# A gated mix of attention and a state-space convolution on one core: wide Toeplitz loads, paired lag steps, 32-channel tables

## The chip, the core and the metric

The kernel runs on one core of one Trainium2 chip. A core has a matrix engine (TensorE, PE in the profile; its weight loads are listed apart as PEld), a vector engine (VectorE, DVE), a scalar engine (ScalarE, ACT), GpSimd (POOL), a queue engine that issues the transfers (SyncE, SP), and 16 DMA engines between HBM and the on-chip memory SBUF, which has 128 partitions. TensorE writes to PSUM, eight banks of 512 float32 columns in each partition. The metric is device time in microseconds of one launch.

## The reference: what is computed

Two branches read the same input x (2048 tokens of 448 channels, bfloat16) and are mixed by a gate of one number per token.

```python
def _A_ref(x, wq, wk, wv, wo):            # attention, 16 heads of 28, one K and one V for all heads
    q = (x @ wq).reshape(B, S, H, Dh).transpose(0, 2, 1, 3)
    k = x @ wk
    v = x @ wv
    scores = einsum("bhqd,bkd->bhqk", q, k) * (Dh ** -0.5)
    p = softmax(scores, axis=-1)
    o = einsum("bhqk,bkd->bhqd", p, v)
    return o.transpose(0, 2, 1, 3).reshape(B, S, H * Dh) @ wo

def _B_ref(u, A_re, A_im, B_re, B_im, C_re, C_im, log_dt, Dskip):   # state-space convolution
    dt = exp(log_dt)[:, None]
    logdA = dt * (A_re + 1j * A_im)       # 448 channels x 256 modes
    dB = dt * (B_re + 1j * B_im)
    P = exp(logdA[:, :, None] * arange(L))
    K = einsum("dn,dnl,dn->dl", C_re + 1j * C_im, P, dB).real   # a kernel of 2048 lags per channel
    y = causal_convolution(u, K)          # by FFT in the reference
    return y + u * Dskip

g = sigmoid((x * gate_w).sum(-1, keepdims=True))
out = g * A_ref(x, ...) + (1 - g) * B_ref(u, ...)
```

In the kernel both branches take their input from x (`A_x`), as the reference does: `b = _B_ref(x, ...)`.

## The kernel before

The program is a list of operations with costs that its author estimated; a scheduler in the kernel file orders them at build time, one fixed order for each engine. Attention is a stream of 1024 score tiles (128 keys x 512 queries of one head). Tiles are scored in batches of three and two alternately, in two halves of three PSUM banks; one exp of ScalarE handles a batch; P.V follows per batch, each head in its own 32-column strip of TensorE, and V carries a column of ones that yields the denominator.

```python
        def qk(b):                       # scores of batch b (3 or 2 tiles), then exp
            for k, (qc, g, kt, h) in enumerate(ts):
                e.matmul(psS[1536 * s + 512 * k : +512], kT[32 * h : +29, 128 * kt : +128], qT[32 * h : +29, ...],
                         tile_position=(32 * h, 0))
            activation(expT[1536 * es], psS[1536 * s], AF.Exp, scale=SQ)                 # "L915" in the profile
        def pv(b):                       # P.V of batch b
            for k, (qc, g, kt, h) in lst:
                e.matmul(psB[32 * h : +32], vaug[32 * kt : +32], expT[1536 * es + 512 * k],
                         start=(kt == 0), stop=(kt == 15), tile_position=(0, 32 * h))    # "L929"
        # ... [cut] order of the program: pv(b), then qk(b + 2)
```

The SSM works on chunks of 16 channels. `masters` squares the mode multipliers z (float32), `tables` builds on VectorE powers of z by doubling (five levels) and, by a sixth step, tables for the second half of the lags; `kgen` multiplies the tables on TensorE into 2048 lags of each channel, which go to an HBM scratch `KP_scratch`. From there each group of four channels comes back as a Toeplitz operand T, a megabyte in two transfers of 64 partitions, in a ring of three buffers. The convolution takes 16 lag steps for each of four channels, each step one matmul of 64 columns:

```python
    def tload(self, gi):
        pg.dma([(self.T.v(64 * h, 64, s * 4096, [[1, 4096]]),
                 dram(self.KP, 4 * gi * KPW + 4096 * h, [[4, 64], [1, 4096]])) for h in range(2)],
               (128, 8192), f"T{s}", rd=[("KP", c), "pad"], wr=[("T", s)], pr=1)
    def conv(self, c):
        for k in range(4):
            self.tload(4 * c + k)
            for m_ in range(16):
                for j in range(4):
                    e.matmul(ps.v(32 * j, 32 - m_, po + 64 * k, [[1, 64]]),
                             self.U.v(0, P, m_ * D + 4 * gi + j, [[D, 32 - m_]]),
                             self.T.v(0, P, s * 4096 + (960 - 64 * m_) * 4 + j, [[4, 64]]),
                             start=(m_ == 0), stop=(m_ == 15), tile_position=(0, 32 * j))   # "L820"
        # ... [cut] one VectorE product by (1 - g) into cst, transposes to token order, added to O ("L828", "L797", "L804")
    def tables(self, c):                 # 28 chunks; per level three products/sums of 4*w*32 elements
        for lv in range(5):
            tensor_tensor(dst3, src, mbf_re, mult)      # "L725"
            tensor_tensor(tmp, src, mbf_im, mult)       # "L728"
            tensor_tensor(dst, dst, tmp, add)           # "L733"
        # then three of 2048 elements for the other half ("L741", "L743", "L748")
```

The gate is computed as a row in all partitions, `grow` = g and `omg` = 1 - g over 2048 tokens. P.V results are multiplied by g as they leave PSUM (`norm`, "L874"); the denominators go through three small transfers (SBUF to SBUF, to HBM, and back as a broadcast) for a reciprocal on 128 partitions. The skip term is x scaled in place by Dskip and 1 - g on VectorE (`bx`, "L837") and added by identity matmuls in the output projection ("L855").

Of the kernel before, what the change touches and what calls it, by code (L numbers as in the profile page):

```python
# [20 lines left out]
CH = 16  # L21
NCH = D // CH
HC = 2 * CH
KPW = 2112
SQ = 1.0 / math.sqrt(DH)
# [28 lines left out]
class Prog:  # L54
# [12 lines left out]
    def op(self, eng, fn, ns, rd=(), wr=(), pr=0, lat=60, lock=None, unlock=None, comm=None):  # L67
# [5 lines left out]
        if comm is not None:  # L73
            deps[self.lastw[comm]] = 1
            self.commops.setdefault(comm, []).append(o.i)
# [36 lines left out]
    def schedule(self):  # L112
# [19 lines left out]
        while done < n:  # L132
            best = None
            for e in ENG:
                T = free[e]
                for i in ready[e]:
                    o = ops[i]
                    r = max(rt[i], T)
                    if o.lock is not None:
                        L = locks.setdefault(o.lock, [None, 0.0, []])  # L140
                        if L[0] is not None:
                            continue
                        r = max(r, L[1])
                    if o.comm in comm:
                        r = max(r, ops[comm[o.comm]].end)
                    key = (r, o.pr, i)
                    if best is None or key < best[0]:
                        best = (key, e, i)
# [10 lines left out]
            if o.comm is not None:  # L159
                if o.comm in comm:  # L160
                    o.deps[comm[o.comm]] = 1
                comm[o.comm] = i
# [124 lines left out]
class Kernel:  # L287
# [10 lines left out]
    def build(self):  # L298
        nc = self.nc
        with self.es:  # L300
# [6 lines left out]
            self.prep_attn()  # L307
# [5 lines left out]
    def alloc(self):  # L313
# [13 lines left out]
        self.GW = sb("GW", NT * P, BF)  # L327
        self.Wb = sb("Wb", P, BF)
        self.ident = sb("ident", P, BF)
        self.absq = sb("absq", 2 * 512, BF)  # L330
        self.qT = sb("qT", 3 * 512, BF)
        self.expT = sb("expT", 3 * 1536, BF)
        self.acc = sb("acc", 2 * 512, F32)
        self.rdenB = sb("rdenB", 512, F32)
        self.denT = sb("denT", 2 * 16, F32)
        self.onT = sb("onT", 8 * 512, BF)
        self.grow = sb("grow", S, BF)
        self.omg = sb("omg", S, BF)
        self.omq = sb("omq", 64, F32)
        self.anti = sb("anti", P, BF)  # L340
        self.U = sb("U", 32 * D, BF)
        self.O = sb("O", 16 * D, BF)
        self.tab = sb("tab", 2 * 6 * 32 * HC, BF)
        self.tmp = sb("tmp", 2 * 2048, BF)
        self.NTR = 3
        self.T = sb("T", self.NTR * 4096, BF)
        self.NB = 7
        self.BC = NCH // self.NB
        self.LV = 256
        self.MC = 5 * 256 + 128  # L350
        self.mbf = sb("mbf", 2 * self.BC * self.MC, BF)
        BW = self.BC * HC
        self.BW = BW
        self.mst = sb("mst", 2 * 2 * BW, F32)
        self.msq = sb("msq", 2 * BW, F32)
        self.sgn = sb("sgn", 8, F32)
        self.seedz = sb("seedz", 2 * 2 * D, F32)
        self.seedw = sb("seedw", 2 * 2 * D, BF)
        self.dt32 = sb("dt32", D, BF)
        self.kstg = sb("kstg", 2 * 256, BF)  # L360
        self.cst = sb("cst", 2 * 256, BF)
        self.small = sb("small", 32, F32)
        self.smallb = sb("smallb", 16, BF)
# [3 lines left out]
    def consts(self):  # L367
        pg = self.pg
        V = lambda b, off, n: b.v(0, P, off, [[1, n]])
        pg.op("pool", lambda e: e.memset(V(self.ident, 0, P), 1.0), 200, wr=["id"])  # L370
# [3 lines left out]
        sm = self.small  # L374
        pg.op("dve", lambda e: e.tensor_reduce(V(sm, 0, 1), self.ident.v(0, P, 28, [[32, 4]]), AX.X, ALU.max),
              100, rd=["id"], wr=["s0"])
        pg.op("dve", lambda e: e.tensor_scalar(V(sm, 1, 1), V(sm, 0, 1), -0.5, 0.5, ALU.mult, ALU.add),
              100, rd=["s0"], wr=["s1"])
        pg.op("dve", lambda e: e.tensor_scalar(V(sm, 2, 1), V(sm, 0, 1), 0.5, 0.5, ALU.mult, ALU.add),
              100, rd=["s0"], wr=["s2"])  # L380
        pg.op("dve", lambda e: e.memset(V(sm, 3, 1), 0.5 * math.pi), 60, wr=["hpi"])
        for c, val in enumerate([-1.0, 1.0, 1.0, -1.0]):
            pg.op("pool", lambda e, c=c, val=val: e.memset(V(self.sgn, c, 1), val), 60, wr=["sgn"])
        ms = lambda buf, n, val, key: pg.op("dve", lambda e: e.memset(V(buf, 0, n), val), 60 + n / 3.8, wr=[key])
        ms(self.Wq, NT * 512, 0.0, "Wq")
        ms(self.Wk, NT * P, 0.0, "Wk")
        pg.op("dve", lambda e: e.memset(self.Wk.v(96, 32, 3 * P + 28, [[32, 4]]), 1.0), 60, wr=["Wk"])
        pg.op("dve", lambda e: e.memset(self.Wk.v(96, 16, 3 * P + 28, [[32, 4]]), 0.0), 60, wr=["Wk"])
        pg.op("dve", lambda e: e.memset(self.xT.v(96, 32, 3 * S, [[1, S]]), 1.0), 600, wr=["xT3a", "xT3b"])
        ms(self.Wo, NT * D, 0.0, "Wo")  # L390
        ms(self.Wb, P, 0.0, "Wb")
        pg.op("dve", lambda e: e.memset(self.vaug.v(0, P, 28, [[32, 16]]), 1.0), 80, wr=["va"])
        pg.op("dve", lambda e: e.memset(self.vaug.v(0, P, 29, [[32, 16], [1, 3]]), 0.0), 80, wr=["va"])
        pg.op("dve", lambda e: e.memset(self.U.v(0, 64, 16 * D, [[1, 16 * D]]), 0.0), 2000, wr=["Uz"])
        an = self.anti.v(0, 32, 0, [[32, 4], [1, 32]])
        pg.op("pool", lambda e: e.memset(an, 1.0), 100, wr=["anti"], pr=4)
        pg.op("pool", lambda e: e.affine_select(out=an, in_=an, compare_op=ALU.is_equal, fill=0.0, base=-31,
                                                pattern=[[0, 4], [1, 32]], channel_multiplier=1), 300,
              rd=["anti"], wr=["anti"], pr=4)
        pg.op("dve", lambda e: e.memset(V(self.kstg, 0, 256), 0.0), 100, wr=[("kst", 0)])  # L400

    def loads(self):
        pg, ins = self.pg, self.ins
        xst = self.tab
        x = ins["A_x"]
        for hf in range(4):
            pg.dma([(xst.v(0, P, hf * 4 * D, [[D, 4], [1, D]]), dram(x, hf * 4 * P * D, [[D, P], [P * D, 4], [1, D]]))],
                   (512, 896), f"x{hf}", wr=[("xst", hf)], eng="sp")
        raw = self.O
        self.names = ["B_A_re", "B_A_im", "B_B_re", "B_B_im", "B_C_re", "B_C_im"]  # L410
        wst = self.acc.cast(BF)
        wks = self.rdenB.cast(BF)

        def lraw(k):
            pg.dma([(raw.v(0, DT, k * 1024, [[NM, 4], [1, NM]]), dram(ins[self.names[k]], 0, [[NM, DT], [DT * NM, 4], [1, NM]]))],
                   (448, 512), f"raw{k}", wr=[("raw", k)])
        pg.dma([(wks.v(0, DT, 0, [[DH, 4], [1, DH]]), dram(ins["A_wk"], 0, [[DH, DT], [DT * DH, 4], [1, DH]])),
                (self.Wv.v(0, DT, 0, [[32, 4], [1, DH]]), dram(ins["A_wv"], 0, [[DH, DT], [DT * DH, 4], [1, DH]]))],
               (896, 56), "wk", wr=["wks", "Wv"])
        pg.op("dve", lambda e: e.tensor_copy(self.Wk.v(0, DT, 0, [[32, 16], [1, DH]]),  # L420
                                             wks.v(0, DT, 0, [[DH, 4], [0, 4], [1, DH]])), 300, rd=["wks"], wr=["Wk", "rd"])
        lraw(0)
        lraw(1)
        pg.dma([(self.dt32.v(0, P, 0, [[1, D]]), dram(ins["B_log_dt"], 0, [[0, P], [1, D]]))], (128, 896), "ldt", wr=["dt"])
        pg.dma([(wst.v(0, DT, 0, [[D, 4], [1, D]]), dram(ins["A_wq"], 0, [[D, DT], [DT * D, 4], [1, D]]))],
               (448, 896), "wq", wr=["wqs"])
        pg.op("dve", lambda e: e.tensor_copy(self.Wq.v(0, DT, 0, [[32, 64], [1, DH]]),
                                             wst.v(0, DT, 0, [[DH, 64], [1, DH]])), 1000, rd=["wqs"],
              wr=["Wq", ("acc", 0), ("acc", 1)])
# [3 lines left out]
        for k in range(2, 6):  # L433
            lraw(k)
# [601 lines left out]
```

## Time and profile before

| | |
|---|---|
| device time, median of 3 runs | 828.8 us (826.26 to 830.79) |
| span of the profiled execution | 814.4 us |
| mean granted TensorE clock | 0.747 of full |
| data moved by DMA | 134.23 MB, mean 165 GB/s |
| Toeplitz loads (T<-KP_scratch) | 224 transfers of 512 KB, median 9.0 us from issue to landing |
| exps (expT<-psS) | 410, mean 1237 ns, 490.7 us busy |

How to read the page: its first part gives each engine's busy time and share; the second cuts the span into 40 slices, in tenths of busy (PEclk is the TensorE clock that was granted, DMA the busy share of the 16 DMA engines); the fourth follows the work that ended last back from the last instruction to what released it, and gives shares by line; the fifth lists groups of instructions with count, busy time, mean duration of one, and the idle time of the engine ahead of them, with what ended it. Matmuls overlap in their pipeline, so group sums exceed the engine's busy time. "L915" is a line of the kernel file. Views by stretch give, for a window of time, each engine's busy time and count of instructions, the clock, the DMA share and the rate.

### The profile page before, as it was taken

To read this page: it belongs to the slowest core of one execution; us is meant where nothing else is said; L and a number is where in the kernel's file an instruction comes from. 1 tells how busy PE (TensorE), PEld (TensorE's weight loads), DVE (VectorE), ACT (ScalarE), POOL (GpSimd) and SP (SyncE) were. 2 spreads that over 40 slices of the span, in tenths; PEclk is the share of its full clock that TensorE was granted. 3 is DMA by queue.
4 is the path that set the end of the run, shared out by engine and by line. 5 is a ranking of instruction groups with operands and counts; after the bars stand their busy time and mean duration, and the time that the engine had idled before them with its cause. 6 is when DMAs were issued, how large, how long until landed. Compare 5 with 4: busy or idle time off the path is not lost.

```text
span 814.4 us, 25556 instructions
## 1 busy us (share of the span) xinstructions
PE 636.6 (78%) x11649; PEld 307.7 (38%) x11649; DVE 530.4 (65%) x1156; ACT 506.6 (62%) x430; POOL 1.6 (0%) x12
## 2 busy tenths in 40 slices
PE   6378888797889878878789978778878988866852
PEld 4212243344334443444443543343433544433211
DVE  7999677956678684956769786755759867300101
ACT  3368667675665755756577856555658766654850
POOL 0000000000000000000000000000000000000000
PEclk9655668687677976868887967775868987876656
DMA  8032883899947899599948799796983799999003
GB/s 209 1 78 59 179 189 85 191 203 209 224 97 165 190 221 225 126 222 210 225 110 201 166 218 221 165 215 136 228 195 95 159 205 214 209 210 214 20 2 103
DMA packets 46036, 134.23 MB, mean 165 GB/s; under 512 B 14968, under 2 KB 29544, under 8 KB 31592
## 3 DMA queue, kind: packets, MB, share of 16 engines
q1 hardware_dynamic: 45928, 132.60, 72.5%
q8 instruction: 91, 1.49, 0.9%
q14 instruction: 17, 0.14, 0.1%
HBM read 128.57 MB, written 3.86 MB: 163 GB/s over the span
## 4 chain that ended last, share of the span: by engine, by line
DMA 38%; PE 38%; DVE 9%; SPq 6%; ACT 5%; issue 4%
DMA T<-KP_scratch 30%; PE psS L820 10%; PE psS L905 9%; PE psB L929 9%; SPq L102 6%; PE psX L764 5%; ACT expT L915 5%; DMA denT<-acc 4%; PE psX L640 2%; DMA rdenB<-R_scratch 2%; DMA R_scratch<-denT 1%; DMA KP_scratch<-kstg 1%; PE psX L851 1%; DVE tab L725 1%; DVE acc L874 1%
## 5 line engine op out<-in xcount | busy, mean ns | idle before, releaser
L915 ACT ACTIVATE expT<-psS 128x1536 bf16<-128x1536 f32 (+1 forms) x410 | 490.7, 1237 | 254.2 <-PE psS L905 247.9
L820 PE MATMUL psS<-T,U 128*32 128x64 bf16 (+15 forms) x7168 | 191.1, 257 | 95.3 <-DMA T<-KP_scratch 70.5
L929 PE MATMUL psB<-expT,vaug 128*32 128x512 bf16 x1024 | 207.4, 494 | 23.4 <-ACT expT L915 18.5
L820 PEld LDWEIGHTS psS<-T,U 128*32 128x32 bf16 (+15 forms) x7168 | 155.5, 182 | 174.3 <-issue 76.6
L905 PE MATMUL psS<-qT,kT 29*128 29x512 bf16 x1024 | 198.1, 484 | 4.2 <-issue 3.8
L905 PEld LDWEIGHTS psS<-qT,kT 29*128 29x128 bf16 x1024 | 39.8, 94 | 147.4 <-issue 146.6
L929 PEld LDWEIGHTS psB<-expT,vaug 128*32 128x32 bf16 x1024 | 53.0, 116 | 71.3 <-ACT expT L915 53.9
L725 DVE TENSOR_TENSOR tab<-tab,mbf 128x2048 bf16<-128x2048 bf16 (+4 forms) x140 | 78.2, 564 | 0.5
L733 DVE TENSOR_TENSOR tab<-tab,tmp 128x128 bf16<-128x128 bf16 (+4 forms) x140 | 77.9, 564 | 0.5
L728 DVE TENSOR_TENSOR tmp<-tab,mbf 128x128 bf16<-128x128 bf16 (+4 forms) x140 | 78.0, 563 | 0.0
L764 PE MATMUL psX<-tab 128*32 128x64 bf16 x1792 | 65.5, 293 | 8.3 <-issue 6.0
L764 PEld LDWEIGHTS psX<-tab 128*32 128x32 bf16 x1792 | 47.8, 140 | 26.6 <-issue 20.3
L828 DVE TENSOR_TENSOR cst<-psS,omq 128x256 bf16<-128x256 f32 x28 | 11.7, 420 | 63.7 <-PE psS L820 63.7
L879 DVE RECIPROCAL denT<-denT 128x16 f32<-128x16 f32 x16 | 4.0, 253 | 54.8 <-DMA denT<-acc 54.6
L883 DVE TENSOR_TENSOR onT<-acc,rdenB 128x512 bf16<-128x512 f32 x16 | 11.0, 690 | 38.9 <-DMA rdenB<-R_scratch 38.9
L874 DVE TENSOR_TENSOR acc<-psB,grow 128x512 f32<-128x512 f32 x16 | 11.0, 689 | 36.4 <-PE psB L929 36.2
L743 DVE TENSOR_TENSOR tmp<-tab,mbf 128x2048 bf16<-128x2048 bf16 x28 | 34.1, 1217 | 0.0
L748 DVE TENSOR_TENSOR tab<-tab,tmp 128x2048 bf16<-128x2048 bf16 x28 | 34.1, 1217 | 0.0
L741 DVE TENSOR_TENSOR tab<-tab,mbf 128x2048 bf16<-128x2048 bf16 x28 | 34.0, 1216 | 0.0
L697 DVE TENSOR_TENSOR mbf<-mst,sgn 128x256 bf16<-128x256 f32 x70 | 29.2, 417 | 0.0
L774 DVE CAST kstg<-psX 128x256 bf16<-128x256 f32 x28 | 11.7, 419 | 22.7 <-PE psX L764 22.5
L646 DVE TENSOR_REDUCE absq<-psX 128x512 bf16<-128x512 f32 x16 | 11.0, 688 | 23.5 <-PE psX L640 23.3
(106 smaller groups left out, 328.7 us busy)
## 6 DMA issues: line engine op xcount, KB each, us to landing
T<-KP_scratch SPq DMA_DIRECT2D x224, 512.0 KB, 9.0
rdenB<-R_scratch SPq DMA_DIRECT2D x64, 64.0 KB, 3.6
U<-in_A_x_dram SPq DMA_DIRECT2D x48, 56.0 KB, 2.2
tab<-in_A_x_dram SPq DMA_DIRECT2D x4, 448.0 KB, 5.0
KP_scratch<-kstg SPq DMA_DIRECT2D x112, 16.0 KB, 4.7
out_dram<-O SPq DMA_DIRECT2D x16, 112.0 KB, 1.8
denT<-acc SPq DMA_DIRECT2D x64, 2.0 KB, 3.7
acc<-in_A_wq_dram SPq DMA_DIRECT2D x1, 392.0 KB, 5.2
```

Of the source, the lines that this page charges most:

```text
L102: return [e.dma_start(o, i, **kw) for o, i in pairs]
L725: pg.op("dve", lambda e, d=dst3, a=src, m=m, w=w: e.tensor_tensor(d, a, mbf.v(0, P, m, [[HC, 4], [0, w], [1, HC]]), ALU.mult), el(n, 1.92) ...
L728: pg.op("dve", lambda e, a=src, m=m, w=w: e.tensor_tensor(tmp.v(0, P, so, [[w * HC, 4], [HC, w], [1, HC]]), a, mbf.v(0, P, m + 128, [[HC, ...
L733: pg.op("dve", lambda e, d=d2, t=t2: e.tensor_tensor(d, d, t, ALU.add), el(n, 1.92), rd=[("tmp", s), ("tab", s, lv + 1)], wr=[("tab", s, l ...
L741: pg.op("dve", lambda e: e.tensor_tensor(dst, src, mbf.v(0, P, m, [[HC, 2], [0, 32], [1, HC]]), ALU.mult), el(n, 1.92), rd=rk + mk, wr=[(" ...
L743: pg.op("dve", lambda e: e.tensor_tensor(tmp.v(0, P, so, [[BLK, 2], [HC, 32], [1, HC]]), src, mbf.v(0, P, m + 64, [[HC, 2], [0, 32], [1, H ...
L748: pg.op("dve", lambda e: e.tensor_tensor(d2, d2, t2, ALU.add), el(n, 1.92), rd=[("tmp", s), ("tab", s, 6)], wr=[("tab", s, 6)], pr=pr)
L764: r = e.matmul(self.psX.v(32 * g, 32, 64 * jj, [[1, 64]]), tab.v(0, P, to + (4 + comp) * BLK + o, [[HC, 32]]), tab.v(0, P, to + comp * BLK ...
L820: r = e.matmul(ps.v(32 * j, 32 - m_, po + 64 * k, [[1, 64]]), self.U.v(0, P, m_ * D + 4 * gi + j, [[D, 32 - m_]]), self.T.v(0, P, s * 4096 ...
L905: r = e.matmul(self.psS.v(0, P, 1536 * s + 512 * k, [[1, 512]]), kT.v(32 * h, DH + 1, 128 * kt, [[1, 128]]), qT.v(32 * h, DH + 1, 512 * qs ...
L915: pg.op("act", lambda e: e.activation(expT.v(0, P, 1536 * es, [[1, n]]), self.psS.v(0, P, 1536 * s, [[1, n]]), AF.Exp, scale=SQ), 172 + n ...
L929: r = e.matmul(self.psB.v(32 * h, 32, 0, [[1, 512]]), vaug.v(0, P, 32 * kt, [[1, 32]]), expT.v(0, P, 1536 * es + 512 * k, [[1, 512]]), sta ...
```

## The change

The change rewrites the SSM, the shape of the P.V groups, the gate, and start and end. Its parts:

- **Toeplitz loads on 128 partitions.** The two transfers of 64 partitions become one of 128, with the lag's two halves in neighbouring partitions; U, the matching layout of x, is loaded the same way.
- **Paired lag steps.** The convolution takes two lag steps at once: 8 matmuls of 128 columns for each channel where there were 16 of 64. The pair's two halves land in two column ranges and are added by the transposes to token order, which double in number.
- **32-channel tables with conjugate negative powers.** 14 chunks; w is multiplied by z^32 once in `masters`; the powers of negative exponent come from the positive ones as conjugate times |z|^-2k (a real table rho).
- **P.V by four heads**, each group all four 32-column strips; exp buffers become a ring of ten tiles; scores of batch s are issued ahead of the P.V of batch s - 2.
- **Gate per token.** The gate's dot product rides in V's projection as a 29th column; g is applied when the output projection is added to the result, as one number per partition. Dskip is added to lag 0 of the convolution kernel, so `bx` and the identity matmuls go.
- **Start and end.** K, V and Q are computed as quarters of x arrive; memsets move to GpSimd; the last denominator is inverted and spread with TensorE transposes instead of transfers.

```diff
-        pg.dma([(self.T.v(64 * h, 64, s * 4096, [[1, 4096]]),
-                 dram(self.KP, 4 * gi * KPW + 4096 * h, [[4, 64], [1, 4096]])) for h in range(2)],
+        pg.dma([(self.T.v(0, P, s * 4096, [[1, 4096]]),
+                 dram(self.KP, 4 * gi * KPW, [[4, 64], [4096, 2], [1, 4096]]))],
...
-            for m in range(0, 16, 2):
...
-                            r = e.matmul(ps.v(32 * j, 32 - m_, po + 64 * k, [[1, 64]]),
-                                         self.U.v(0, P, m_ * D + 4 * gi + j, [[D, 32 - m_]]),
-                                         self.T.v(0, P, s * 4096 + (960 - 64 * m_) * 4 + j, [[4, 64]]),
+            for n in range(8):
...
+                        r = e.matmul(ps.v(32 * j, 32 - 2 * n, po + 128 * k, [[1, 128]]),
+                                     self.U.v(0, P, 2 * n * D + 4 * gi + j, [[D, 32 - 2 * n]]),
+                                     self.T.v(0, P, s * 4096 + (896 - 128 * n) * 4 + j, [[4, 128]]),
...
-CH = 16
-NCH = D // CH
+NC = D // 32
...
+        vo(lambda e: e.tensor_tensor(tab.v(0, P, FM, [[64, 2], [EW, 32], [1, 64]]),
+                                     tab.v(0, P, lo + 31 * EW, [[BLK, 2], [-EW, 32], [1, 64]]),
+                                     rho.v(0, P, 31 * 64, [[0, 2], [-64, 32], [1, 64]]), ALU.mult), 4096, ...)
+        ni = tab.v(0, P, lo + BLK + EW, [[EW, 31], [1, 64]])
+        vo(lambda e: e.tensor_scalar(ni, ni, -1.0, None, ALU.mult), 31 * 64, ...)
...
+        def pv(v):
+            ts = range(4 * v, 4 * v + 4)
+                for t in ts:
+                    r = e.matmul(self.psB.v(32 * h, 32, 0, [[1, 512]]), vaug.v(0, P, 32 * kt, [[1, 32]]),
+                                 expT.v(0, P, 512 * (t % 10), [[1, 512]]), ...)
...
+        for s in range(len(sets)):
+            qk(s)
+            if s >= 2:
+                while nv < NTL // 4 and 4 * nv + 3 <= sets[s - 2][-1]:
+                    pv(nv)
...
-            for T in range(NT):
-                r = e.matmul(t.v(0, P, o + DT * T, [[1, DT]]), self.xT.v(...), self.ident.v(0, DT, 0, [[1, DT]]), ...)
+        e.scalar_tensor_tensor(ov, px, self.gt.v(0, P, tl, [[1, 1]]), ov, ALU.mult, ALU.add)
```

## The prediction

> **What bounds the kernel now.** I read the page from the top: engine busy shares, the 40 slices, the chain that ended last, the costliest groups.
>
> ```profile
> PE 636.6 (78%) x11649; PEld 307.7 (38%) x11649; DVE 530.4 (65%) x1156; ACT 506.6 (62%) x430; POOL 1.6 (0%) x12
> ...
> PEclk9655668687677976868887967775868987876656
> DMA  8032883899947899599948799796983799999003
> ...
> DMA 38%; PE 38%; DVE 9%; SPq 6%; ACT 5%; issue 4%
> DMA T<-KP_scratch 30%; PE psS L820 10%; PE psS L905 9%; PE psB L929 9%; SPq L102 6%; PE psX L764 5%; ACT expT L915 5%; DMA denT<-acc 4%; PE psX L640 2%; DMA rdenB<-R_scratch 2%; DMA R_scratch<-denT 1%; DMA KP_scratch<-kstg 1%; PE psX L851 1%; DVE tab L725 1%; DVE acc L874 1%
> ...
> L915 ACT ACTIVATE expT<-psS 128x1536 bf16<-128x1536 f32 (+1 forms) x410 | 490.7, 1237 | 254.2 <-PE psS L905 247.9
> L820 PE MATMUL psS<-T,U 128*32 128x64 bf16 (+15 forms) x7168 | 191.1, 257 | 95.3 <-DMA T<-KP_scratch 70.5
> L929 PE MATMUL psB<-expT,vaug 128*32 128x512 bf16 x1024 | 207.4, 494 | 23.4 <-ACT expT L915 18.5
> ```
>
> No engine is full. The last chain is carried by two things, the Toeplitz loads (30%) and TensorE (38%). The exps, the largest single piece of work, wait 247.9 us for score matmuls: TensorE executes in order, so a convolution that waits for its load holds up the scores behind it. The next view is busy time by stretch (columns: stretch, length, PE, PEld, DVE, ACT, POOL, clock, DMA share, GB/s).
>
> ```profile
> 54.00:76.00 22.00, 18.12 (x84) 3.36 (x79) 21.59 (x58) 18.96 (x17) 0.00 (x0) 0.50 0.31 83
> 80.00:760.00 680.00, 556.49 (x11123) 278.23 (x11121) 453.47 (x987) 439.00 (x367) 0.00 (x0) 0.77 0.83 183
> 540.00:560.00 20.00, 12.87 (x270) 6.34 (x264) 9.03 (x20) 9.38 (x9) 0.00 (x0) 0.66 1.03 225
> ...
> 3.00:8.00 5.00, 3.56 (x32) 3.47 (x33) 3.89 (x5) 1.14 (x2) 0.00 (x0) 1.00 1.11 348
> ```
>
> I count in sets: one exp of 1536 columns (1453 ns) and one of 1024 (1023 ns), five score tiles. There are 1024 / 5 = 204.8 sets, and ACT alone needs 2.48 us for each, 507 us in all: the floor of both kernels. From 80 to 760 us, with the SSM beside the attention, 367 exps ran: 183.5 sets at 3.71 us. TensorE is busy 3.03 us of that and waits 0.67. Between 540 and 560 us the DMA engines are full (share 1.03) at only 225 GB/s, while the start, loading x and weights into 112 and 128 partitions, reached 348 GB/s. Where attention runs alone, the chain of waits repeats every 2.71 us:
>
> ```profile
> 766.57 1.46 ACT expT L915
> 768.03 0.04 issue
> 768.08 0.61 PE psB L929 x3
> 768.69 0.57 PE psS L905 x3
> 769.26 0.02 issue
> 769.28 1.46 ACT expT L915
> ```
>
> An exp, then the P.V that reads it, then the scores that refill its banks: P.V stands between exp and scores and costs ACT 0.23 us a set.
>
> **What the Trainium skill says.** "SBUF — State Buffer", section "Door 1: The DMA port swizzle (why `[64,N]` ≈ `[32,N]`)": partitions 0 to 63 reach 8 of 16 ports, asymptote about 218 GB/s, all 128 about 436 (196 against 328 measured at 1 MiB). The trace agrees on the first: 225 GB/s with full engines. "DMA: Bandwidth & Descriptors", section "Rules for kernel authors": two transfers to disjoint partition halves serialize; use one of 128 partitions. That is this change. "TensorE: Matmul & The Clock Gate", section "Back-to-back issue gap": a matmul of 64 columns or fewer costs an issue floor of some 25 ns, whatever its columns. L820 shows 191.1 us / 7168 = 26.7 ns each; bursts with a warm clock come lower (56 in 1.28 us including the drain of the last). "VectorE: DVE Perf Modes", section "Side-by-side: where the cycles go for N=2048 bf16": 1224 ns at two elements a cycle; the table products here take 1216.
>
> **The change part by part.**
>
> *Loads.* 112 MB-sized loads either way, 117 MB. At 225 GB/s they need 1.05 MB / 225 = 4.66 us each, 522 us, which fill most of the 660 us in which they run. At some 350 GB/s (the rate of the start) they need 3.0 us each, 336 us. I expect the 70.5 us of direct waits mostly to go, and with them the scores' waits behind. The source pattern (two rows 4096 elements apart for each lag) is new; if the engines share ports in it, the rate may be lower.
>
> *Convolution.* 7168 matmuls of 64 columns become 3584 of 128; the columns streamed stay equal. A quad (four column tiles) took 4 x 26.7 = 107 ns; 128 columns in four tiles at once should take about 110, now limited by streaming at low clock or by issue at high clock. 896 x 0.11 = 99 us against 191: about 92 less.
>
> *P.V by 4 heads.* 410 groups (three or two tiles, running together in separate column tiles) took 207.4 us, 0.506 each. 256 groups of four: 130 us, 77 less. The scores are also issued ahead of the P.V of two sets earlier, so the 2.71 us loop should fall to ACT's own 2.48 to 2.52.
>
> *Gate, skip, output.* Scaling x (16 x 738 ns on DVE), the gate matmuls (3.6 us) and the 64 identity matmuls of the skip (5.4 + 1.9 us) go. The output transposes double in number (10.2 us to about 18). Net about 3 us of PE less, 12 us of DVE less.
>
> *Tables.* Three DVE lines of levels and three of the negative powers sum to 78.2 + 78.0 + 77.9 + 34.1 + 34.1 + 34.0 = 336 us. Per 32 channels they handle 36,100 elements; now 23,800 in the levels, 4,100 for the conjugate product, 2,000 for its real scale and 2,000 at double speed for a sign: about 31,000. So some 290 us, 46 less. With x scaling, start memsets (10 us, to GpSimd) and one pass less in the masters, but a doubled gated copy, DVE comes to about 450 us.
>
> *Start and end.* Before, sustained exps begin at about 51 us, because projections stand behind parameter work and V behind the gate. In the changed order K, V and Q come first. ACT work ahead of the first exp is four x copies (1 us), four K copies (0.6), three parameter functions (0.6 to 1) and two table loads (1.28): about 12 us, after x lands at about 5. With waits: first exp at 22 us. At the end, P.V finished at about 788 and the last instruction at 814: 26 us, three DMA round trips for the reciprocal among them. On TensorE that is some eight steps of 0.3 to 1.2 us and the output DMA: 12 us.
>
> **The sum.** The order of instructions puts the first convolution of the changed kernel behind score tile 120, the last behind 895. So 155 sets have SSM work beside them and about 50 have none. The groups of TensorE overlap in their drains: they sum to some 750 us where the union is 636.6, a factor 0.85. For a set in the SSM stretch: scores 198.1/204.8 = 0.97, P.V 130/204.8 = 0.63, projections and output 0.20, convolution, kernels and transposes (99 + 66 + 18)/155 = 1.18; sum 2.98, times 0.85 = 2.53 us of TensorE, against 2.48 of ACT. Two engines that evenly matched don't overlap perfectly; before, 0.67 us a set were idle, a little over half of it direct load waits. I take 0.27 us: 2.80.
>
> Start 22 + 50 x 2.51 = 126 + 155 x 2.80 = 434 + end 12 = 594 us of span. The measured median stands 14.4 us above the span now (828.8 against 814.4): 608 us.
>
> **Rivals.** (a) *DVE becomes the bound.* It must do about 435 us of its 450 before the last convolution ends, by the sum above at 22 + 60 + 434 = 516 us: 86% full. Between 80 and 760 us it was 453/680 = 67% busy, with long waits for psS and denT in its own queue. For it: in-order queue, tables on the path of every kernel. Against it: most of those waits came from late loads. If it reaches only 75%, the SSM ends near 590 and the total is about 660. (b) *The loads stay slow.* If the new pattern gets 225 GB/s, 522 us of loads start at about 75 us; the stretch is about 530 long instead of 434, total some 690. The 348 GB/s at the start speak against it. (c) *The clock.* Attention alone runs at 0.50, the SSM stretch at 0.77. Half as many convolution matmuls may lower it: scores and P.V cost 0.54 us a group cold and 0.32 warm from start to start, so a cold stretch needs above 3.2 us a set: 155 x 0.4 = 62 us more, 670. (d) *Everything overlaps*: ACT never waits, 22 + 507 + 12 + 14 = 555.
>
> **Range and chances.** (d) is an edge I don't expect to be reached, and (a) and (c) in part are likely: 570 to 665. Even (b) is far below 811, so slower needs something I don't see: faster 0.96, same 0.02, slower 0.02.
>
> **What would show it.** Loads right: GB/s above 300 in stretches with a full DMA, and the Toeplitz load below 10% of the last chain. Convolution right: about 100 us in its group with about 110 ns per quad. P.V: about 130 us. Exps: idle below 120 us, and a period of 2.5 us where attention is alone. DVE about 450 us. First exp near 22 us, last P.V to end about 12. Wrong: the exps' wait still near 250 us, the DVE above 85% with TensorE waiting for tables, or DMA full at 225 GB/s.

## The result, and the profile after

The changed kernel takes 669.8 us (median of 4 runs, 664.46 to 673.83) where the kernel before takes 827.5 us beside it: a ratio of 0.814 [0.807, 0.821]. The prediction was 608 us with a range of 570 to 665. Direction and most mechanisms came as described; the gain is 158 us instead of 221, and the time lies above the range.

These are lines of the changed kernel's page: busy times, the granted clock and the DMA share in 40 slices, shares of the chain that ended last, and groups (busy, mean ns | idle before, with what ended most of it).

```profile
PE 553.9 (84%) x8234; PEld 269.0 (41%) x8234; DVE 475.7 (72%) x1045; ACT 498.3 (75%) x427; POOL 19.3 (3%) x24
...
PEclk9955557989899998899798998988988996855556
DMA  9630018787857678578778786878479669530000
...
PE 37%; DMA 29%; DVE 17%; ACT 12%; SPq 3%; issue 1%; DVEq 0%
DMA T<-KP_scratch 18%; ACT expT L986 12%; PE psS L973 9%; PE psS L841 8%; PE psX L799 6%; PE psB L995 6%; DMA denT<-acc 5%; SPq L111 3%; PE psX L649 2%; DVE tab L760 2%; DMA R_scratch<-denT 2%; DVE tmp L761 2%; DMA rdenB<-R_scratch 2%; DVE qT L661 1%; PE psX L878 1%; DVE acc L895 1%
...
L986 ACT ACTIVATE expT<-psS 128x1536 bf16<-128x1536 f32 (+1 forms) x410 | 483.5, 1255 | 134.4 <-PE psB L995 84.8
L973 PE MATMUL psS<-qT,kT 29*128 29x512 bf16 x1024 | 189.4, 458 | 43.2 <-ACT expT L986 42.1
L841 PE MATMUL psS<-T,U 128*32 128x128 bf16 (+7 forms) x3584 | 156.8, 307 | 31.7 <-DMA T<-KP_scratch 28.1
L995 PE MATMUL psB<-expT,vaug 128*32 128x512 bf16 x1024 | 111.7, 464 | 1.7 <-DVE acc L895 1.7
```

The exps wait 134.4 us instead of 254.2, and what they wait for has changed: 84.8 us now end with a P.V matmul (psB), where before 247.9 us ended with a score matmul. An exp doesn't read psB. What it needs of P.V is the exp buffer that P.V reads: it may not overwrite it earlier. The convolution has half as many matmuls and yet 156.8 us, 43.8 ns each. The waits for T fell from 70.5 to 28.1 us.

By stretch (length; PE, PEld, DVE, ACT, POOL busy; clock; DMA share; GB/s), the first with the convolutions beside the attention, the second attention alone; then ten microseconds in which the DMA engines are full:

```profile
116.00:579.00 463.00, 411.10 (x7229) 221.85 (x7219) 368.35 (x808) 359.13 (x304) 0.00 (x0) 0.92 0.75 257
579.00:648.00 69.00, 51.48 (x281) 9.80 (x281) 5.08 (x9) 58.55 (x51) 0.00 (x0) 0.50 0.10 29
...
240.00:250.00 10.00, 7.46 (x138) 3.85 (x135) 9.77 (x13) 9.16 (x8) 0.00 (x0) 1.00 0.99 362
```

304 exps are 152 sets (a set is two exps, five score tiles), so a set takes 463 / 152 = 3.05 us there; TensorE is busy 2.70 of it and idle 0.34. Attention alone takes 69 / 25.5 = 2.71 a set, outputs and denominators included. A full DMA moves 362 GB/s: the loads do what they were meant to.

The span in the prediction's terms: first exp at 31 us; 28 sets at 3.04 up to 116 us; 152 at 3.05; 25.5 at 2.71; end 14.7; sum 662.7. Against the 594 predicted, with the sets counted where they fell, that is 9 us at the start, 20 in the sets without convolutions, 38 in those with them, 3 at the end: 69 us of span. In the median the miss is 62, because the prediction added 14.4 us for what the median stands above the span. That was no cost of the kernel: it compared different executions. In every recorded run an execution's device time is 1.7 to 1.8 us above its own span; here the median stands 7.1 us above the profiled span. This term hid 7 us of the miss by luck.

Why attention alone takes longer shows in the chain of what ended last, in order of time (start, length, what):

```profile
596.39 9.15 ACT expT L986 x8
605.54 0.05 issue
605.59 0.61 PE psS L973 x3
606.19 0.58 PE psB L995 x4
606.77 0.02 issue
606.79 9.15 ACT expT L986 x8
```

Eight exps, four sets, run with hardly a pause in 9.15 us: 2.29 a set. That is less than the 2.48 which the prediction took for ScalarE's floor by adding the mean durations of single exps; exps in a row overlap a little. Then ScalarE stands still for 1.26 us: three scores, and behind them four P.V matmuls. The period is 10.41 us, 2.60 a set. The code gives the reason. Call the three or two tiles of one exp a batch. The exp of batch 8 (tiles 20 to 22) overwrites ring places 0 to 2, which hold tiles 10 to 12. Tile 12 belongs to P.V group 3 (tiles 12 to 15), and a group is issued behind the scores of batch s once its last tile lies in batch s - 2 or earlier: tile 15 is in batch 6, so group 3 comes right behind the scores of batch 8. The exp thus waits for its own scores and for a P.V queued after them. Counted through the loop, that holds for 51 of the 410 exps, one in each 20 tiles; the trace has 55 such waits. With 15 places no exp needs a P.V that was issued less than two batches earlier.

### The profile page after: what moved, and what is told of

It reads as the page before. It is cut to its first block, busy times and chain, and to the rows that moved or that the text cites. A ratio compares the mean times of both kernels' runs of the same rounds, so it can differ in the third digit from the quotient of the medians.

```text
span 662.7 us, 18405 instructions
## 1 busy us (share of the span) xinstructions
PE 553.9 (84%) x8234; PEld 269.0 (41%) x8234; DVE 475.7 (72%) x1045; ACT 498.3 (75%) x427; POOL 19.3 (3%) x24
## 3 DMA queue, kind: packets, MB, share of 16 engines
q8 instruction: 64, 1.05, 0.6%
## 4 chain that ended last, share of the span: by engine, by line
PE 37%; DMA 29%; DVE 17%; ACT 12%; SPq 3%; issue 1%; DVEq 0%
DMA T<-KP_scratch 18%; ACT expT L986 12%; PE psS L973 9%; PE psS L841 8%; PE psX L799 6%; PE psB L995 6%; DMA denT<-acc 5%; SPq L111 3%; PE psX L649 2%; DVE tab L760 2%; DMA R_scratch<-denT 2%; DVE tmp L761 2%; DMA rdenB<-R_scratch 2%; DVE qT L661 1%; PE psX L878 1%; DVE acc L895 1%
## 5 line engine op out<-in xcount | busy, mean ns | idle before, releaser
L986 ACT ACTIVATE expT<-psS 128x1536 bf16<-128x1536 f32 (+1 forms) x410 | 483.5, 1255 | 134.4 <-PE psB L995 84.8
L973 PE MATMUL psS<-qT,kT 29*128 29x512 bf16 x1024 | 189.4, 458 | 43.2 <-ACT expT L986 42.1
L841 PE MATMUL psS<-T,U 128*32 128x128 bf16 (+7 forms) x3584 | 156.8, 307 | 31.7 <-DMA T<-KP_scratch 28.1
L841 PEld LDWEIGHTS psS<-T,U 128*32 128x32 bf16 (+7 forms) x3584 | 107.7, 155 | 77.8 <-DMA T<-KP_scratch 37.1
L995 PE MATMUL psB<-expT,vaug 128*32 128x512 bf16 x1024 | 111.7, 464 | 1.7 <-DVE acc L895 1.7
L760 DVE TENSOR_TENSOR tab<-tab,mbf 128x4096 bf16<-128x4096 bf16 (+4 forms) x70 | 69.6, 995 | 0.0
L761 DVE TENSOR_TENSOR tmp<-tab,mbf 128x256 bf16<-128x256 bf16 (+4 forms) x70 | 69.2, 989 | 0.0
L995 PEld LDWEIGHTS psB<-expT,vaug 128*32 128x32 bf16 x1024 | 22.8, 97 | 64.0 <-issue 59.2
L776 DVE TENSOR_TENSOR tab<-tab,rho 128x4096 bf16<-128x4096 bf16 x14 | 32.0, 2288 | 0.0
L649 PE MATMUL psX<-xT,Wq 112*128 112x512 bf16 x64 | 22.5, 451 | 5.8 <-DVE Wq L440 5.8
L684 DVE TENSOR_TENSOR msq<-mst 128x256 f32<-128x256 f32 x63 | 27.1, 430 | 0.0
L772 DVE TENSOR_TENSOR rho<-rho,mbf 128x64 bf16<-128x64 bf16 (+4 forms) x70 | 25.4, 363 | 0.0
```

Source lines behind the costliest of these rows:

```text
L649: pg.op("pe", lambda e, T=T: e.matmul(px, self.Wq.v(0, DT, T * 512 + g * 128, [[1, 128]]), self.xT.v(0, DT, T * S + 512 * qc, [[1, 512]]), ...
L684: pg.op("dve", lambda e, k=k: e.tensor_tensor(msq.v(0, P, 0, [[BW, 2], [1, BW]]), both(k - 1), both(k - 1), ALU.mult), el(2 * BW), rd=keys ...
L760: vo(lambda e, dst=dst, src=src, mr=mr: e.tensor_tensor(dst, src, mr, ALU.mult), 2 * n, done + mk(lv), [kr, ki])
L761: vo(lambda e, src=src, mi=mi, w=w: e.tensor_tensor(tmp.v(0, P, 0, [[w * EW, 2], [EW, w], [1, EW]]), src, mi, ALU.mult), 2 * n, done + mk( ...
L776: vo(lambda e: e.tensor_tensor(tab.v(0, P, FM, [[64, 2], [EW, 32], [1, 64]]), tab.v(0, P, lo + 31 * EW, [[BLK, 2], [-EW, 32], [1, 64]]), r ...
L841: r = e.matmul(ps.v(32 * j, 32 - 2 * n, po + 128 * k, [[1, 128]]), self.U.v(0, P, 2 * n * D + 4 * gi + j, [[D, 32 - 2 * n]]), self.T.v(0, ...
```

## The experiments

Theory: in the changed kernel the exp ring of ten tiles, not the amount of work of any engine, sets the pace of the middle; the start lost to memsets is a second, separate loss. Rivals: the convolution that costs 157 us instead of 99 (TensorE's work), VectorE's tables, the loads, the clock.

**Where the gain came from: the wide loads alone, and all the rest without them.**

```diff
 # b_wide: the kernel before, T (and U's matching layout) as one transfer of 128 partitions
+        pg.dma([(self.T.v(0, P, s * 4096, [[1, 4096]]), dram(self.KP, 4 * gi * KPW, [[4, 64], [4096, 2], [1, 4096]]))],
 # e_narrow: the changed kernel, T and U as two transfers of 64 partitions each
+        pg.dma([(self.T.v(64 * h, 64, s * 4096, [[1, 4096]]), dram(self.KP, 4 * gi * KPW + 4096 * h, [[4, 64], [1, 4096]])) for h in range(2)],
```

> The kernel before with one part of the change alone: each Toeplitz load is one transfer of 128 partitions (lag halves in neighbouring partitions, U laid out to match, its zeroed half cleared on all partitions); the order of instructions is kept, the computation is complete. Theory (the loads held the kernel before): the rate in the convolution stretch rises from 225 GB/s to above 280, the direct waits of L820 for T fall from 70 us to below 25, and the time falls by 60 to 110 us, to 720 to 770. Rival (TensorE and the attention loop held it, the loads were only the last of several things to arrive): the waits for T go but the time falls by less than 25 us, to above 805.

> The changed kernel with its loads undone: T comes again in two transfers of 64 partitions, U laid out to match; all else stays. Theory (the wide loads are what lets the rest of the change pay): 225 GB/s again, 112 loads need 522 us from about 98 us on, so the last convolution ends after 620 us instead of 579 and the time rises by 40 to 90 us, to 710 to 760. Rival (TensorE and VectorE now set the pace, loads have slack): less than 2% more, below 683.

Measured: b_wide 699.3 us, ratio 0.855 [0.853, 0.857]; e_narrow 809.1, ratio 0.989 [0.987, 0.991]. From b_wide, exps and convolution; then the same of e_narrow, each from its list of groups:

```profile
L916 ACT ACTIVATE expT<-psS 128x1536 bf16<-128x1536 f32 (+1 forms) x410 | 488.5, 1238 | 138.4 <-PE psS L906 130.7
L821 PE MATMUL psS<-T,U 128*20 128x64 bf16 (+15 forms) x7168 | 185.4, 253 | 35.0 <-DMA T<-KP_scratch 23.8
```

```profile
L985 ACT ACTIVATE expT<-psS 128x1536 bf16<-128x1536 f32 (+1 forms) x410 | 486.6, 1252 | 276.3 <-PE psS L972 143.0
L840 PE MATMUL psS<-T,U 128*32 128x128 bf16 (+7 forms) x3584 | 162.8, 308 | 127.4 <-DMA T<-KP_scratch 120.7
```

The loads of e_narrow in a stretch with full DMA engines:

```profile
300.00:400.00 100.00, 75.27 (x1244) 38.56 (x1243) 65.30 (x154) 60.68 (x52) 0.00 (x0) 0.71 0.94 206
```

With wide loads the T waits of the kernel before fall from 70.5 to 23.8 us and the exps' from 247.9 to 130.7; over three quarters of the whole gain (0.145 of 0.186) is this one line. Without it everything else is worth 1%: the DMA engines are 94% busy at 206 GB/s between 300 and 400 us, and T is 33% of the last chain. Both expectations were too small: b_wide falls by 119 us where 60 to 110 were expected, and e_narrow lies above its 710 to 760. The other parts count only once the loads are out of the way; parts of a change whose gains hide one another can't be added up singly.

**The exp ring.**

```diff
-        self.expT = sb("expT", 10 * 512, BF)
+        self.expT = sb("expT", 15 * 512, BF)        # and t % 10 -> t % 15 throughout
-        self.rho = sb("rho", 32 * 64, BF)
+        self.rho = self.tmp                         # makes room; wks gets a tile of its own
-                  wr=[X, ("b", 2 + tt)], pr=1)
+                  wr=[X, ("b", 2 + tt)] + ([("cx", c) for c in range(28)] if tt == 3 else []), pr=1)
```

The last two edits are the side conditions of the first; e_alias has them and keeps the ring at ten.

> The changed kernel with a ring of 15 exp tiles instead of ten (the room comes from putting the table rho into the buffer tmp; the last output bank waits for all convolutions). An exp can then start without waiting for the P.V that is issued after the next scores. Theory (the ring is what holds the exps, 84.8 us of waits for psB): these waits fall below 20 us, exps run in 2.5 us a set where attention is alone, and the time falls by 20 to 40 us, to 630 to 650. Rival (TensorE, VectorE and ScalarE are all nearly full in the SSM stretch, so the waits of the exps are only where the balance shows): the exps' waits move to the scores, convolutions are left over behind the last scores, and the time stays within 10 us of 670.

> The two side edits of the larger ring alone: the phase table put into the scratch of the products, and the last output bank taken only after every convolution; the ring stays at ten. If the ring is what the 24.6 us came from, this is as the changed kernel, 665 to 675 us, with the exps' waits for psB still near 85 us. If a side edit (another order of issue) did it, this goes towards 645.

Measured: e_ring15 645.2 us, ratio 0.788 [0.782, 0.793]; e_alias 674.4, ratio 0.822 [0.815, 0.830], with 87.2 us of exps waiting for psB. The exps' waits (in total, times, longest), of the changed kernel and then of e_ring15:

```profile
ACT expT L986 <- PE psB L995: 84.8, 55, 3.4
ACT expT L986 <- PE psS L973: 47.5, 72, 3.7
```

```profile
ACT expT L987 <- PE psS L974: 85.8, 116, 3.9
ACT expT L987 <- PE psB L996: 1.1, 1, 1.1
```

The waits for psB are gone, as expected, and the kernel is 24.6 us faster. Less than the 84.8 us comes back, since the waits for scores grow by 38. The ring did it and the side edits did not.

**The start.** The changed kernel moved two large memsets to GpSimd. One timeline of it shows the first of them beside a VectorE instruction; the second fence is the same instruction with the memsets back on VectorE (e_dvememset):

```profile
8.57 6.38 POOL L374 MEMSET U<- 128x7168 bf16 x1
8.97 6.22 DVE L579 TENSOR_SCALAR rdenB<-cst 128x448 f32<-128x448 bf16 x1
```

```profile
9.67 0.40 DVE L579 TENSOR_SCALAR rdenB<-cst 128x448 f32<-128x448 bf16 x1
```

```diff
-        pm(V(self.U, 16 * D, 16 * D), 0.0, 6000, ["U"], 5)                # GpSimd
+        pg.op("dve", lambda e: e.memset(V(self.U, 16 * D, 16 * D), 0.0), 2000, wr=["U"])
 # and the memset of O in the same way
```

> The changed kernel with the two large memsets (U and O) back on VectorE. Theory (GpSimd's memsets lock VectorE out: the tensor_scalar L579 took 6.2 us beside the memset of U, three instructions 4 to 5 us each beside the memset of O): L579 falls below 1 us, the first exp starts at about 26 us instead of 31, and the time falls by 5 to 12 us. Rival (VectorE has slack at that point and the memsets now take its own time, about 6 us): within 3 us of 670.

Measured: 665.2 us, ratio 0.812 [0.808, 0.816]. VectorE's 0.4 us instruction, issued 0.4 us after the GpSimd memset, takes 6.22 us and ends 0.24 us after it, and everything in VectorE's queue stands behind it. The Trainium skill's page "SBUF — State Buffer", section "Who interferes with whom", says that a `tensor_scalar` can enter a mode that uses two ports, and that VectorE in such a mode and GpSimd lock each other out for a whole instruction; this trace agrees. The first exp moves from 30.95 to 26.5 us. The total moves by no more than its intervals allow: the waits for psB behind it grow from 84.8 to 92.0 us.

**Both together**, each edit as above:

> The ring of 15 exp tiles and the two memsets back on VectorE, together. If the two causes are separate (exps that wait for their ring in the middle, VectorE locked out at the start), their gains add: 24.6 and 4.6 us below 669.8, so about 641 us, first exp near 26.5 us. If both only feed the same later wait (convolutions behind the last scores), the end swallows the 4.6 us and it stays at 645.

Measured: 631.0 us (628.25 to 635.36), ratio 0.770 [0.766, 0.775], faster than both kernels and some 10 us below what the two single gains add up to (both expectations, 641 and 645, were too high; why the two together give more is open). Its exps, convolution, and the stretch that took 304 exps in the changed kernel:

```profile
L987 ACT ACTIVATE expT<-psS 128x1536 bf16<-128x1536 f32 (+1 forms) x410 | 484.7, 1254 | 76.2 <-PE psS L974 71.7
L842 PE MATMUL psS<-T,U 128*32 128x128 bf16 (+7 forms) x3584 | 158.4, 305 | 41.1 <-DMA T<-KP_scratch 36.7
```

```profile
116.00:579.00 463.00, 416.88 (x6969) 216.01 (x6975) 369.07 (x804) 402.24 (x339) 0.00 (x0) 0.91 0.68 234
```

339 instead of 304 exps in the same 463 us, 2.73 us a set instead of 3.05. The whole convolution costs as much as before (158.4 us), but not all of it stands in this stretch: 3116 of its matmuls against 3511, and 384 come after 579 us, where few exps are left.

**Is it TensorE's work?** Half of the convolution matmuls left out (the output lacks every second pair of lag blocks), once with the ring of ten and once with the ring of 15.

```diff
-            for n in range(8):
+            for n in range(0, 8, 2):
```

> The changed kernel with every second convolution matmul left out (1792 of 3584: the output lacks half of the lag blocks), the loads and tables as they are. It takes some 78 us off the convolution's 156.8. If TensorE's time in the SSM stretch sets the total, the exps' idle time falls and 45 to 80 us go: 590 to 625 us. If the wait for the exp ring and the loads set it, under 25 us go: 645 us or more. If the granted clock falls with the work taken off, as when the strided reads were made contiguous, the remaining matmuls grow and it lies between.

> The kernel of 631 us (ring of 15, memsets on VectorE) with every second convolution matmul left out (the output lacks half of the lag blocks). Halving them did nothing while the exps waited for the ring. If the ring hid TensorE's load, it counts now: 580 to 605 us. If the clock takes it back or VectorE's tables and the loads set the pace, 620 us or more, with the clock below 0.80.

Measured: with the ring of ten 675.8 us, ratio 0.823 [0.821, 0.826]: nothing gained, at a group 69 us shorter. With the ring of 15: 613.5 us, ratio 0.746 [0.740, 0.752], 17.5 us less than the 631.0 and between its two expectations. From e_halfconv's page:

```profile
PEclk9955557768577886887586877785958987555556
...
L986 ACT ACTIVATE expT<-psS 128x1536 bf16<-128x1536 f32 (+1 forms) x410 | 483.7, 1251 | 145.2 <-PE psB L995 85.6
L841 PE MATMUL psS<-T,U 128*20 128x128 bf16 (+3 forms) x1792 | 88.2, 311 | 44.6 <-DMA T<-KP_scratch 42.9
```

The waits for psB stay, at 85.6 us. The mean clock falls from 0.828 to 0.719 (with the ring of 15 from 0.849 to 0.771), so that scores cost 208.6 us instead of 189.4 and P.V 124.5 instead of 111.7. Part of the work taken off comes back as a slower clock, so these runs tell what leaving the work out brings, not what a faster convolution at an unchanged clock would.

**Why the convolution costs 44 ns a matmul.** T's columns read contiguously, or U's (the values are then not the reference's, the amount of work is the same), and each matmul issued as two of 64 columns (part of the first lag step is probably not kept in the sum):

```diff
 # e_tcont
-    self.T.v(0, P, s * 4096 + (896 - 128 * n) * 4 + j, [[4, 128]])
+    self.T.v(0, P, s * 4096 + 1024 * j + 896 - 128 * n, [[1, 128]])
 # e_ucont
-    self.U.v(0, P, 2 * n * D + 4 * gi + j, [[D, 32 - 2 * n]])
+    self.U.v(0, P, 2 * n * D + 32 * (gi % 3) + 128 * j, [[1, 32 - 2 * n]])
 # e_split64
+    for hc in range(2): matmul(ps.v(32 * j, 32 - 2 * n, po + 128 * k + 64 * hc, [[1, 64]]), U..., T.v(..., [[4, 64]]))
```

> The changed kernel, but the convolution's moving operand is read as 128 neighbouring elements instead of every fourth one; the convolution's values are then not the reference's, all counts and shapes stay. Question: why 3584 matmuls of 128 columns take 156.8 us (43.8 ns each) and not the 99 us of the prediction. Theory (reading with a step of four elements slows the stream): L841 falls to 90 to 115 us, and the time by 10 to 30 us. Rival (the load of a new weight tile for every matmul sets the pace): L841 stays above 145 us and the time within 1.5%.

> The changed kernel, but the convolution's weights are read as neighbouring elements instead of with a step of 448; the convolution's values are then not the reference's, all counts and shapes stay. Theory (the weight loads set the pace, and the wide step makes them slow): the weight loads of L841 fall below 80 us from 107.7 and the matmuls with them to below 130 us. Rival (the moving operand's step sets the pace, or the count of instructions): L841 stays above 145 us and the time within 1.5%.

> The changed kernel with the pairing undone in its count alone: each convolution matmul of 128 columns is issued as two of 64 with the same weights, 7168 in all, with the same sums and an unchanged order. Theory (each matmul has a floor beside its columns): L841 rises from 157 to 180 to 200 us, as before the change, and the time by 10 to 35 us. Rival (the columns alone count): L841 stays within 155 to 170 us and the time within 1.5%.

Measured: e_tcont 680.9 us, ratio 0.833 [0.830, 0.835], its convolution 129.5 us (36.1 ns each); e_ucont 667.9 us (656.24 to 669.36; three of its four executions, the profiled one too, lie over 1.5% above the fastest, so no ratio is given), convolution 144.4 us (40.3 ns each); e_split64 695.2, ratio 0.850 [0.845, 0.856], convolution 181.2 us, 25.3 ns for each half. From e_tcont:

```profile
PEclk9755665688557775897797997785669895555556
...
L973 PE MATMUL psS<-qT,kT 29*128 29x512 bf16 x1024 | 209.1, 505 | 44.4 <-ACT expT L986 43.0
L841 PE MATMUL psS<-T,U 128*32 128x128 bf16 (+7 forms) x3584 | 129.5, 279 | 29.9 <-DMA T<-KP_scratch 24.8
```

So of the 43.8 ns some 8 go with the stride of four in T and some 3.5 with the stride in U. Each theory foresaw more: with contiguous T a convolution of 90 to 115 us, with contiguous U weight loads below 80 us, where they came to 86.5 from 107.7. Without T's stride the convolution saves 27 us, but the clock is 0.708, scores cost 209.1 us instead of 189.4, and the kernel is slower. Pairing is still worth its place: taken back, it costs 25 us.

**Is it VectorE?** The negative powers worked out for the first 32 channels only; the other 416 are left with what stands in the tables.

```diff
+        if c >= 1:                       # leave out rho, the conjugate product and the sign
+            ...
+            return
```

> The changed kernel with VectorE work left out: the real table rho, the conjugate product and the sign (L772, L776, L781 and the copy beside them) are computed for the first of the 14 chunks only, so later convolution kernels are wrong. About 65 us of VectorE work goes. Theory (VectorE, 80 to 92% busy in the SSM stretch, sets the pace): the time falls by 30 us or more, to below 640. Rival (TensorE with the convolution's real cost and the exps' ring set it): less than 12 us, to above 656.

> The kernel of 631 us with the conjugate part of the tables worked out for the first 32 channels only (values of the others wrong), some 54 us less on VectorE, which is busy over 90% between 200 and 500 us. If VectorE is the bound once the ring isn't, kernels, loads and convolutions come earlier and the convolutions left behind the last scores shrink: 590 to 615 us. If TensorE's order or its clock is the bound, 622 to 635 us.

Measured: 671.7 us, ratio 0.820 [0.817, 0.824] at a VectorE of 421.8 us; with the ring of 15, 630.2, ratio 0.766 [0.760, 0.773]. Some 55 us less of VectorE change neither kernel.

**The order of issue.** In e_ring15_dvems the last convolutions come after the last score. Three priorities on top of that kernel (the transposes to token order go with the convolutions):

```diff
-                      ... conv ... pr=4        # kgen pr=1.7
+                      ... conv ... pr=0.6      # e_ring15_convfirst
+                      ... conv ... pr=-1       # e_ring15_tabfirst, kgen pr=-1
+                      ... conv ... pr=1.5      # r15d_mild, kgen pr=1.2
```

> As the run before, and convolutions ahead of scores in the order of issue, so that the last convolution stands behind score tile 808 instead of behind the last. If the last 25 to 40 us of the larger ring were lost because TensorE had left convolutions over for a time without scores, this gives them back: 615 to 630 us. If TensorE's own work is what counts (550 us busy wherever it stands) or the loads then come too late for the convolutions, the exps wait in the middle instead: 640 us or more, with the exps' idle time again above 110 us.

> As the run before, with the kernels' matmuls ahead of the scores too, which spreads both evenly over score tiles 130 to 835. If late kernels and late loads hold the convolutions up, this beats the version with convolutions alone ahead, by 5 to 15 us. If the convolutions ahead of scores only move the wait to the exps, it is no better: 640 us or more.

> The kernel of 631 us with the convolutions a little earlier in the order: the last behind score tile 950, neither bunched ahead of the scores (700.9) nor left behind the last of them (631). If the stretch without scores at the end is loss, it takes off half of it: 615 to 627 us. If any convolution ahead of scores stops the exps through the ring or a late load, 632 us or more.

Measured: 700.9 us, ratio 0.854 [0.850, 0.858]; 664.4, ratio 0.809 [0.806, 0.813]; 635.9, ratio 0.772 [0.765, 0.779]. None gains; moving the kernels' matmuls ahead too takes back 36 of the 70 us that the convolutions alone lost. ScalarE's waits in e_ring15_convfirst (in total, times, longest):

```profile
ACT expT L987 <- PE psB L996: 96.3, 3, 50.9
ACT expT L987 <- PE psS L974: 80.5, 108, 3.0
```

The exps stand still for 44 and 51 us at a stretch. In the first of these (250 to 294 us) TensorE ran 416 convolution and 192 kernel matmuls, 8 of P.V and 3 scores, and its convolutions waited 11.3 us for T: the order had put a block of SSM work in front of a P.V group, and the exps ran into the end of their ring. The convolutions left behind the last score are not plain loss; in none of the three orders did moving them ahead of it pay.

These orders also leave attention alone at the end, with the ring of 15. From e_ring15_tabfirst, to be set beside the stretch from 579 to 648 us of the changed kernel, which has as many exps at the same clock:

```profile
590.00:650.00 60.00, 49.75 (x261) 9.73 (x261) 4.56 (x8) 57.37 (x51) 0.00 (x0) 0.50 0.04 10
```

The 51 exps take 60 us instead of 69, 2.35 a set instead of 2.71.

## Why the prediction was wrong

*The loads: right.* 1.05 MB at 362 GB/s is 2.9 us, 3.0 was predicted; the direct waits went from 70.5 to 28.1 us, and with the wide loads alone (b_wide) the exps' waits for scores from 247.9 to 130.7. The condition set for the last chain (below 10%) did not come: T is still 18% of it. That share reads which wait ended last, not what a faster load would bring. Rival (b) is refuted by the 362 GB/s; e_narrow shows what slow loads cost, 809 us, far above the 690 that the rival reckoned with.

*The loop: the step that failed.* The prediction wrote: "The scores are also issued ahead of the P.V of two sets earlier, so the 2.71 us loop should fall to ACT's own 2.48 to 2.52." It looked at what the new order takes out of the loop, and not at what the ring of ten tiles puts in: one exp in eight needs a P.V issued behind its own scores. Attention alone runs at 2.60 a set for that, where ScalarE alone needs 2.29; with the ring of 15 it took 2.35, outputs included. The floor of 2.48 a set, 507 us in all, was wrong as well: the page of the kernel before has the exps busy for 490.7 us, because their single durations overlap. With the SSM beside it, convolution, kernel or projection matmuls also run in 36 of the 40 waits for psB between 116 and 579 us; over all 55 waits the average is 84.8 / 55 = 1.5 us, the longest 3.4. Before that stretch, from 31 to 116 us, the ring counts too: 61 exps in e_ring15 where the changed kernel has 56. The 0.27 us of idle that the prediction added to a set came out as 0.34, on top of a busier TensorE. With the ring of 15 the kernel lies at 645 us, inside the range, and with the start mended at 631: 39 of the 62 us by which the time lies above 608.

*The convolution: the largest term mis-sized, and not shown to be the cause.* 896 quads at 0.110 us were to be 99 us; they are 156.8, or 0.175. The prediction took four column tiles to share one stream of 128 columns and the step to cost an issue each. It costs 43.8 ns against 25.3 for 64 columns, so columns still count, and a stride of four goes with 8 of it. The 58 us too many stand in TensorE's 2.70 us a set, predicted as 2.53. But the ring of 15 alone brings the kernel into the range with the convolution at 158.7 us, and with the ring of ten half of the convolution left out gains nothing. Part of that is lost to the slower clock: whether 99 us at an unchanged clock would also have brought the time down to 665 no run shows. With the ring of 15 the same halving is worth 17.5 us: then the term begins to count. Two smaller misses point the other way, by luck: P.V at 111.7 us for 130, scores at 189.4 for 198.1.

*The first exp: wrong by 9 us.* 22 us predicted, 31 measured. 4.5 of the 9 are the GpSimd memset that locks VectorE out; the rest, in the chain of K, V and Q, I have not taken apart.

*Tables and end: nearly right.* VectorE 475.7 us for 450; the last stretch 14.7 for 12.

*Rival (a), VectorE*, refuted: 55 us less of it gains nothing, though it is 80% busy in the stretch with convolutions. *Rival (c), the clock*: the feared fall did not come in the changed kernel, 0.92 in that stretch against 0.77 before, with a TensorE that waits less. It came in the experiments: with half the convolution and with contiguous T.

What is left between 631 and 608 is not settled: half the convolution gives 17.5 us of it, VectorE and the order of issue none.

## What to carry to other kernels

For each ring of buffers, write down for every producer which consumer must have read the place, and where that consumer stands in its engine's order relative to the producer's own inputs; a ring that is one group too short shows up as a wait for a result the producer never reads. The largest miss in a sum need not be the cause: test whether leaving the work out moves the time before blaming it. Busy time taken off TensorE can come back as a lower clock, as in two runs here: look at the clock of such a run before reading its time.

## What the runs showed of the hardware

- Two runs with less convolution work showed a lower granted clock of TensorE: 0.719 with half the convolution, 0.708 with contiguous T reads, 0.828 in the changed kernel. It is no rule: with contiguous U, 12 us less of convolution, it was 0.81 to 0.84. Attention alone stays at 0.50 with TensorE busy 51.48 of 69 us.
- A moving operand with a stride of four bf16 costs 43.8 ns for 128 columns, a contiguous one 36.1, in four column tiles, at a lower clock at that.
- U's weights read at a stride of 448 elements load in 155 ns on average, contiguous in 105, and the convolution takes 144.4 us instead of 156.8; the effect on the kernel's time is unclear (656 to 669 us).
- A GpSimd memset of 7168 bf16 in each partition takes 6.4 us; a 0.4 us tensor_scalar of VectorE that started 0.4 us after it ended 0.24 us after its end.
